# A fused mLSTM cell and feed-forward kernel: another order for the first chunk, the first weight quarter converted in halves, and 60 spare products

## The chip, the cores and the metric

The kernel runs on one core of one Trainium2 chip. A core has TensorE (PE: matrix products, with its weight loads shown as PEld), VectorE (DVE), ScalarE (ACT), GpSimd (POOL) and SyncE (SP), which here does nothing but issue DMAs. The metric is the device time of one execution in microseconds (us). Before the change the median of three runs is 491.05 us (490.83 to 491.35).

## The reference

Two layers follow each other. The first is an mLSTM cell: 4 batches, 8 heads, 768 time steps, head dimension 40. The second is a feed-forward block on its output, 3072 rows of 320 values.

```python
for t in range(S):
    m_new = max(f[t] + m, i[t])
    f_stab = exp(f[t] + m - m_new); i_stab = exp(i[t] - m_new); m = m_new
    C = f_stab * C + i_stab * outer(v[t], k[t])
    n = f_stab * n + i_stab * k[t]
    h = C @ q[t]
    y[t] = sigmoid(o[t]) * h / max(abs(n . q[t]), 1)
...
x = y.transpose(0, 2, 1, 3).reshape(B * S, H * D)
h = x @ w_in
out = max(0.01 * h, h) @ w_out
```

`w_in` is 320 x 2048 and `w_out` 2048 x 320. In this kernel both arrive as 64-bit floating point numbers and are converted on the chip.

## The kernel before

The 768 time steps are cut into six chunks of 128 (called c or g, 0 to 5); a step s is one batch of one chunk, s = 4c + b. Inside a chunk the cell is done with products: scores of k and q, a mask of decay factors from the gates, values, and the state that goes on to the next chunk. Each chunk's output (four steps of 128 rows) is one group for the feed-forward block. While group g goes through the feed-forward block, the cell of chunk g + 1 is worked in between its units.

Chunk 0 has nothing to be hidden behind. Its order is written out by hand in the string `ORDER` (lines 1102 to 1119), which `first_chunk` (line 1121) reads item by item. Inside `tc.manual_schedule` (line 1152) each of PE, DVE, ACT and POOL executes its instructions in the order in which the program issues them, and SP's queue has the program's order too. The items, with the batch as their first number:

- `ld`: load k, q, v (SP, line 368). `lo`: load the output gate (line 397). `lw n`: load piece n of the weights (line 230 for `w_in`, line 235 for `w_out`).
- `g`, `ge`, `ug`: the gates' scans on DVE (lines 293 to 313), their exponentials on ACT (319 to 325), their transposition on PE into the bank `tg` (342, 347), copied by DVE (352, 354).
- `ab n`: spread the gate sums over the partitions, two batches at once (PE, 461); `abw`: add the causal mask (DVE, 471); `exp`: eight exponentials of 128 x 128 (ACT, 488).
- `tr b i`, `tc b i`: transpose k (i = 0) or q (i = 1) on PE (578), copy the result on ACT (584). `sc`: scores (PE, 593); `scm`: multiply them into the mask (DVE, 600).
- `vu`: v times gate (POOL, 498); `st`: the state's products (PE, 608); `stc`: its copy (DVE, 616).
- `val`: values, eight products of 41 columns into the bank `pa` (PE, 673); `den`: denominators (DVE, 665 to 667); `o`: tanh of the output gate (ACT, 524); `gate`: gate times values (DVE, 685); `gp`: scaling by the denominators (POOL, 702).
- `x`: transpose the result (PE, 876, 877); `xc`: copy it to `xT` in four pieces (ACT, 889, 890).
- `nw n`: one further step of converting weight piece n. `narrow_weights` (line 248) is a generator: its first step is an absolute value on ACT (260), and six steps on DVE follow (262, 264, 266, 271, 275, 277).
- `ff n`: a unit of the feed-forward block (products at line 907, leaky relu on ACT at 915).
- `warm n`: n products of the identity with itself into one bank, whose result nobody reads (336).
- `fd s`: load of a step of chunk 1 (`load` and `spread`, lines 370, 377, 440); `ll s i`: a late part of it (411); `ps`, `tiles`: memsets on POOL.

PE writes into eight PSUM banks: four with the tag "mm" (pool `psf`: `warm`, `ab`, `ph`, `po`) and four with the tag "c" (pool `psc`: `tkq`, `sc`, `dC`, `pa`, `tg`, `xt` and the cell's). A bank is given out in turn, and its first writer waits for the last reader of the use before.

`w_in` is kept as four quarters (n = 0 to 3), each 128 partitions x 1280 and each loaded by ten DMAs; quarter n serves the feed-forward's pairs of row blocks j = 2n and 2n + 1, of which the even one uses the first and the odd one the second 128 columns of each of the five slots of 256. `w_out` is kept as eight pieces (n = 4 to 11) of 128 x 640. Quarters 0 and 1 lie, before their conversion, in parts of `acts` not yet in use, quarters 2 and 3 in `raw_t`.

Behind `first_chunk` stands a loop over the feed-forward units of group 0 (lines 1153 to 1200). For unit i it first takes `PASSES[i]` steps of weight conversion (pieces 2 to 11), asks for further pieces of `w_out` by `fetch`, issues the unit, and then as many units of chunk 1's cell as `place` says: the m-th of them goes behind unit `place[m]`. The units of the cell are, for each batch, `u_parts` (lines 634 to 661: scores and the state of the chunk's halves, `sd`) and `u_plain` (706 to 730: the values, bank `hN` at line 713), then the gates of chunk 2 between them, and last `u_x1` for the four batches. After this loop groups 1 to 5 follow, from line 1276 on.

In group 0 the feed-forward units before are fourteen half units of 256 columns (two batches) behind the two of the first chunk, then sixteen parts of the second product (`part`, line 938: four products of 320 columns), 30 in all.

Of the kernel before, what the change touches and what calls it, by code (L numbers as in the profile page):

```python
# [22 lines left out]
def kernel(  # L23
# [27 lines left out]
    B, H, S, D = q.shape  # L51
    P = 128
# [15 lines left out]
    NF = FF // P  # L68
    GT = B * P
    KF = Dm // P  # L70
    KR = Dm - KF * P
    KC = Dm // DP
# [4 lines left out]
    gp = ctx.enter_context(tc.tile_pool(name="gates", bufs=1))  # L77
# [96 lines left out]
    def f_of(r, j):  # L174
        n, e = divmod(j, 2)
        return 4 * n + 2 * r + e
# [8 lines left out]
    raws = {}  # L185
# [51 lines left out]
    def halves(n, size):  # L237

        flat = late_t[:].rearrange("p n t -> p (n t)")
        if n < QN:  # L240
            at = flat[:, n % 2 * (WC // 2) :]
        elif n % 2 == 0:
            at = xb[:].rearrange("p n d -> p (n d)")
        else:
            at = flat[:, 2 * H * SL :]
        return at[:, : size // 2].bitcast(BF16)

    def narrow_weights(n):

        if not wide:
            return
        raw, dst = raws.pop(n)
        words = raw.bitcast(U32).rearrange("p (c two) -> p c two", two=2)
        lo, hi = words[:, :, 0], words[:, :, 1]
        tops = raw.bitcast(BF16).rearrange("p (c four) -> p c four", four=4)[:, :, 3]
        top = halves(n, dst.shape[1])
        t = top.bitcast(U16)
        nc.scalar.activation(top, tops, AF.Abs)  # L260
        yield
        nc.vector.tensor_scalar(top, top, scalar1=2.0**-15, scalar2=130560.0, op0=ALU.max, op1=ALU.min)
        yield
        nc.vector.tensor_scalar(t, t, scalar1=0x07F0, scalar2=3, op0=ALU.bitwise_and, op1=ALU.logical_shift_left)
        yield
        nc.vector.scalar_tensor_tensor(  # L266
            t, in0=tops.bitcast(U16), scalar=0xC000, in1=t, op0=ALU.bitwise_and, op1=ALU.bitwise_or,
        )
        yield
        d = dst.bitcast(U32)  # L270
        nc.vector.tensor_scalar(
            d, hi, scalar1=0x000FFFFF, scalar2=0x00100000, op0=ALU.bitwise_and, op1=ALU.bitwise_or,
        )
        yield
        nc.vector.scalar_tensor_tensor(dst, in0=lo, scalar=2.0**-32, in1=d, op0=ALU.mult, op1=ALU.add)  # L275
        yield
        nc.vector.scalar_tensor_tensor(dst, in0=dst, scalar=2.0**-20, in1=top, op0=ALU.mult, op1=ALU.mult)
# [78 lines left out]
    st = {}  # L356
# [540 lines left out]
    def by_slot(t, dt=F32):  # L897
        return t[:].bitcast(dt).rearrange("p b (k t) -> p k b t", t=P)

    def ff_units(g):  # L900
        xT = by_slot(st["xT", g])

        def rows(j, ph, cols, slots):
            bs = slice(cols.start // P, cols.stop // P)
            for slot in slots:
                for r in range(2):
                    nc.tensor.matmul(  # L907
                        ph[r][:, cols], lhsT=w_row(r, slot, j), rhs=xT[DP * r : DP * (r + 1), slot, bs, :],
                        start=(slot == 0), stop=(slot == KC - 1),
                    )  # L910

        def relu(j, ph, cols):
            for r in range(2):
                f = f_of(r, j)
                nc.scalar.activation(acts[:, f, cols], ph[r][:, cols], AF.Prelu, alpha=0.01)  # L915

        def pair(j):
            ph = []

            def first():  # L920
                ph.extend(psf.tile([P, GT], F32, name=f"ph{r}", tag="mm") for r in range(2))
                rows(j, ph, slice(0, GT), range(3))

            def second():
                rows(j, ph, slice(0, GT), range(3, KC))
                relu(j, ph, slice(0, GT))

            return [first, second]

        def half(j, h):  # L930
            ph = [psf.tile([P, GT], F32, name=f"ph{r}", tag="mm") for r in range(2)]
            cols = slice(h * GT // 2, (h + 1) * GT // 2)
            rows(j, ph, cols, range(KC))
            relu(j, ph, cols)

        po = {}

        def part(n, m):
            if m == 0:
                po[n] = psf.tile([P, Dm], F32, name="po", tag="mm")  # L940
            for f in range(m * NF // 4, (m + 1) * NF // 4):
                nc.tensor.matmul(  # L942
                    po[n][:], lhsT=acts[:, f, ts(n, P)], rhs=w_out[:, f, :], start=(f == 0), stop=(f == NF - 1),
                )
            if m == 3:
                if n < 2:
                    y = wk.tile([P, Dm], F32, name="y")[:]
                else:
                    y = wk.tile([P, H, D1], F32, name="hn")[:].rearrange("p h d -> p (h d)")[:, :Dm]
                nc.scalar.copy(y, po[n][:])  # L950
                nc.sync.dma_start(out[n * S + g * P : n * S + (g + 1) * P, :], y)

        if g == 0:

            ins = [(j, h) for j0 in range(0, NF // 2, 2) for h in range(2) for j in (j0, j0 + 1)]
            return [lambda j=j, h=h: half(j, h) for j, h in ins] + [
                lambda n=n, m=m: part(n, m) for m in range(4) for n in range(B)
            ]
        firsts = [u for j in range(NF // 2) for u in pair(j)]
        for n in range(2):  # L960
            firsts[KH + 2 * n] = lambda n=n, u=firsts[KH + 2 * n]: (u(), mix_early(n))
        return firsts, fast_units(g)
# [137 lines left out]
            nc.tensor.matmul(st["warm"][:], lhsT=ident[:], rhs=ident[:], start=True, stop=True)  # L1100

    ORDER = """
ld 0; warm 12; ld 1; ld 2; lo 0; lo 1; lo 2; lw 0
g 0; ld 3; lw 1; lw 2; lo 3; ge 0; ug 0; tr 0 0
tr 0 1; vu 1; vu 0; tc 0 0; ab 0; abw 0; tr 1 0; tc 0 1
exp 0; sc 0; abw 1; tr 1 1; tc 1 1; st 0; tc 1 0; exp 1
st 1; scm 0; stc 1; stc 0; ab 2; tiles; g 1; abw 3
sc 1; scm 1; ge 1; abw 2; val 0; tr 2 0; tr 2 1; val 1
o 1; den 0; tc 2 1; gate 1; ps 1; tc 2 0; o 0; exp 2
gate 0; gp 0; ug 1; sc 2; scm 2; x 0; tr 3 0; nw 0  # L1110
nw 0; vu 2; den 1; gp 1; nw 0; nw 0; nw 0; exp 3
tr 3 1; tc 3 0; ps 0; st 2; tc 3 1; xc 0; val 2; vu 3
sc 3; stc 2; nw 0; o 2; nw 0; nw 1; scm 3; den 2
x 1; xc 1; gate 2; st 3; o 3; gp 2; nw 1; nw 1
stc 3; nw 1; ff 0; val 3; den 3; x 2; gate 3; fd 4
nw 1; ps 3; xc 2; ff 1; gp 3; x 3; nw 1; ll 4 1
xc 3; ps 2; ll 4 2; fd 5; ll 5 1; lw 3; lw 4; lw 5
lw 6; fd 6; fd 7; ll 5 2; nw 1
"""

    def first_chunk():

        ffs, narrow = [], {}

        def ff(n):
            if not ffs:
                ffs.extend(ff_units(0))
            ffs[n]()

        def step(n):  # L1130
            if n not in narrow:
                narrow[n] = narrow_weights(n)
            next(narrow[n], None)
# [15 lines left out]
        return ffs  # L1149

    E = mybir.EngineType
    with tc.manual_schedule(engines={E.PE, E.DVE, E.Activation, E.Pool}):
        ffs = first_chunk()[2:]
        fetch = {6: (3, 4), 17: (7,), 10: (5, 6)}
        PASSES = (3, 2, 1, 0, 3, 5, 3, 1, 0, 1, 4, 2, 3, 4, 1, 2, 8, 4, 5, 4, 5, 4, 0, 7, 3, 5, 5, 1, 2, 8)
        place = (1, 4, 7, 9, 11, 15, 15, 18, 23, 25, 27, 27, 28)
        late = {}
        now = (None for n in range(2, QN + NF // 2) for _ in narrow_weights(n))

# [170 lines left out]
```

## Time and profile before

| | |
|---|---|
| median of three runs | 491.05 us (490.83 to 491.35) |
| the profiled execution: time | 491.28 us |
| its span, first to last instruction | 489.4 us |
| mean granted clock of PE | 0.982 |
| first chunk ends on PE (last transpose of x) | 47.1 us |
| first product of group 1 | 135.24 us |

The page gives each engine's busy time as a share of the span, then the span in 40 equal slices of 12.2 us: a digit is the busy share of a slice in tenths, and in the row PEclk the granted clock of PE. Views of the trace are named in words: the table by stretch gives busy time, number of records, clock and DMA of each engine between two times; the waits say what an engine's idle time ended with; the chain follows the work that ended last back from its end; the timeline lists groups of an engine's instructions with their start and length in us, and in brackets the idle time before them and what ended it. A product of 32-bit numbers shows as two records on PE.

### The profile page before, as it was taken

The page shows a single profiled execution, that of the slowest core. Times are in us where ns is not written, and L with a number is a line of the kernel's source. Part 1 is how long each engine was busy: PE and PEld are TensorE (multiplying, and loading weights), DVE is VectorE, ACT ScalarE, POOL GpSimd, SP SyncE. Part 2 cuts the span into 40 slices and gives each one's busy share as a digit, 9 for nine tenths or more (in the row PEclk, how much of TensorE's full clock was granted, in tenths as well). Part 3 has the DMA queues.
Part 4 walks back from the last instruction along what each step waited for, and adds up shares of the span by engine and source line. Part 5 has one row for each costly group of instructions (what it writes and reads, how often), then busy time and mean ns, then how long its engine had stood idle before and what let it go on. Part 6 is the DMA issues. An engine that isn't in the chain of part 4 may idle for free.

```text
span 489.4 us, 12856 instructions
## 1 busy us (share of the span) xinstructions
PE 476.1 (97%) x5137; PEld 377.9 (77%) x5137; DVE 365.9 (75%) x595; ACT 197.4 (40%) x510; POOL 160.3 (33%) x207
## 2 busy tenths in 40 slices
PE   7969998999999999999999999999999999999997
PEld 6857887777745479975559995557998889988997
DVE  5796999799924999777898777679899968335611
ACT  4674885453642240324342141425024752156310
POOL 4234454070600725817280563644220002100020
PEclk9867999999999999999999999999999999999999
DMA  7777686898623566668787877755151030100001
GB/s 136 177 191 146 161 226 134 216 229 177 143 97 90 133 158 176 162 152 202 152 197 160 189 181 177 184 144 153 44 229 42 1 107 1 42 15 0 1 1 54
DMA packets 142699, 63.41 MB, mean 130 GB/s; under 512 B 110832, under 2 KB 130864, under 8 KB 142640
## 3 DMA queue, kind: packets, MB, share of 16 engines
q1 hardware_dynamic: 142256, 62.47, 52.7%
q8 instruction: 40, 0.66, 0.6%
q14 instruction: 19, 0.16, 0.1%
q10 hardware_dynamic: 384, 0.13, 0.1%
HBM read 51.68 MB, written 8.27 MB: 122 GB/s over the span
## 4 chain that ended last, share of the span: by engine, by line
PE 82%; SPq 8%; DVE 5%; issue 2%; DMA 2%; ACT 1%; ACTq 0%; DVEq 0%
PE po L983 32%; PE ph L907 24%; PE ph L833 8%; PE po L942 6%; PE pe L833 4%; PE pT L743 3%; PE sd L650 3%; SPq L230 3%; SPq L368 2%; SPq L377 1%; PE sd L655 1%; DVE w_in L275 1%; PE hN L713 1%; DMA raw<-in_moe_w_in_dram 1%; DVE late L266 1%
## 5 line engine op out<-in xcount | busy, mean ns | idle before, releaser
L907 PE MATMUL ph<-xT,w_in 64*128 64x512 f32 (+1 forms) x800 | 146.3, 516 | 0.2 <-ACT xT L889 0.2
L907 PEld LDWEIGHTS ph<-xT,w_in 64*128 64x128 f32 x800 | 77.8, 190 | 57.4 <-issue 50.8
L983 PE MATMUL po<-w_out,acts 128*128 128x160 f32 x640 | 91.0, 301 | 0.0
L983 PEld LDWEIGHTS po<-w_out,acts 128*128 128x128 f32 x640 | 87.5, 190 | 3.4 <-ACT w L488 1.5
L915 ACT ACTIVATE acts<-ph 128x512 f32<-128x512 f32 (+1 forms) x80 | 36.8, 508 | 83.6 <-PE ph L907 83.5
L488 ACT ACTIVATE w<-w,gT 128x64 f32<-128x64 f32 (+1 forms) x192 | 52.0, 349 | 29.0 <-POOL w L480 28.0
L628 POOL TENSOR_TENSOR S<-S,f 40x336 f32<-40x336 f32 x36 | 32.5, 902 | 93.3 <-PE pT L743 49.5
L983 PE MATMUL po<-raw,acts 128*128 128x160 f32 x320 | 45.1, 299 | 0.0
L983 PEld LDWEIGHTS po<-raw,acts 128*128 128x128 f32 x320 | 44.0, 190 | 0.0
L660 DVE TENSOR_TENSOR qn<-w,sd 64x512 f32<-64x512 f32 x40 | 27.4, 684 | 21.0 <-PE sd L655 14.0
L1016 POOL TENSOR_TENSOR y<-y,raw 128x160 f32<-128x160 f32 x10 | 5.5, 555 | 112.3 <-ACT y L1015 112.3
L942 PE MATMUL po<-w_out,acts 128*128 128x320 f32 x128 | 36.0, 436 | 0.0
L855 DVE SCALAR_TENSOR_TENSOR acts<-ph,acts 128x512 f32<-128x512 f32 x32 | 20.6, 684 | 20.7 <-ACT acts L853 20.7
L541 DVE TENSOR_TENSOR qn<-kqT,late 64x512 f32<-64x512 f32 x32 | 33.1, 1033 | 1.0
L480 POOL TENSOR_TENSOR w<-w,i 128x512 f32<-128x512 f32 x20 | 31.8, 1591 | 2.7 <-ACT acts L915 1.9
L942 PEld LDWEIGHTS po<-w_out,acts 128*128 128x128 f32 x128 | 23.8, 190 | 9.5 <-issue 0.3
L757 POOL TENSOR_TENSOR xb<-xb,den 128x320 f32<-128x320 f32 x16 | 11.6, 727 | 48.7 <-DVE xb L754 48.7
L853 ACT ACTIVATE acts<-pe 128x512 f32<-128x512 f32 x32 | 17.4, 594 | 19.2 <-PE pe L833 19.0
L761 DVE STREAM_TRANSPOSE x<-xb 128x512 f32<-128x512 f32 x16 | 17.8, 1114 | 7.7 <-POOL xb L757 7.7
L859 ACT ACTIVATE acts<-acts 128x512 f32<-128x512 f32 x32 | 19.7, 633 | 8.0 <-DVE acts L855 8.0
L983 PE MATMUL po<-raw 128*128 128x160 f32 x160 | 22.7, 300 | 0.0
L650 PEld LDWEIGHTS sd<-kqT 40*64 40x64 f32 x640 | 19.7, 135 | 3.7 <-issue 3.0
(166 smaller groups left out, 773.2 us busy)
## 6 DMA issues: line engine op xcount, KB each, us to landing
w<-a_dr SPq DMA_DIRECT2D x40, 128.0 KB, 3.7
rb<-in_k_dram SPq DMA_DIRECT2D x64, 80.0 KB, 3.1
rb<-in_q_dram SPq DMA_DIRECT2D x64, 80.0 KB, 2.7
rb<-in_o_gate_dram SPq DMA_DIRECT2D x64, 80.0 KB, 2.6
xT<-x_dr SPq DMA_DIRECT2D x32, 160.0 KB, 3.2
late<-a_dr SPq DMA_DIRECT2D x32, 128.0 KB, 3.4
x_dr<-x SPq DMA_DIRECT2D x16, 256.0 KB, 3.4
kn<-in_k_dram SPq DMA_DIRECT2D x24, 160.0 KB, 3.7
```

Source lines behind the costliest of these rows:

```text
L480: nc.gpsimd.tensor_tensor(w, w, cm2.unsqueeze(1).to_broadcast([P, H, SL]), op=ALU.add)
L488: yield nc.scalar.activation(w[:, h, :], w[:, h, :], AF.Exp, bias=gT[c][:, 0, bh : bh + 1], scale=1.0)
L541: nc.vector.tensor_tensor(mixed(s)[rows, 1 - r], d["kqT"][rows, 1].rearrange("p (h t) -> p h t", t=SL), d["ea"][rows], op=ALU.mult,)
L628: nc.gpsimd.tensor_tensor(new, old, g, op=ALU.mult)
L650: nc.tensor.matmul(bank[1 - u][toks, h, :], lhsT=kqT[rows, 0, ts(h, SL)], rhs=kqT[rows, 1, ts(h, SL)], start=True, stop=True,)
L660: nc.vector.tensor_tensor(mixed(s)[toks, u], w[toks], bank[1 - u][toks], op=ALU.mult)
L833: nc.tensor.matmul(ph[r][:], lhsT=parts["w", key][n][part, at : at + P], rhs=xs[key][part, slot, :], start=start and slot == 0, stop=stop ...
L855: nc.vector.scalar_tensor_tensor(fs[r], in0=ph[r][:], scalar=1.0 + EPS, in1=fs[r], op0=ALU.mult, op1=ALU.add,)
L907: nc.tensor.matmul(ph[r][:, cols], lhsT=w_row(r, slot, j), rhs=xT[DP * r : DP * (r + 1), slot, bs, :], start=(slot == 0), stop=(slot == KC ...
L915: nc.scalar.activation(acts[:, f, cols], ph[r][:, cols], AF.Prelu, alpha=0.01)
L942: nc.tensor.matmul(po[n][:], lhsT=acts[:, f, ts(n, P)], rhs=w_out[:, f, :], start=(f == 0), stop=(f == NF - 1),)
L983: nc.tensor.matmul(bank[:], lhsT=left[:, f, :], rhs=right[:, f, :], start=f == 0, stop=f == KH - 1)
```

## The change

The order of the first chunk is written anew, in four respects.

- Loads. The first quarter of `w_in` (`lw 0`) stands behind the loads of steps 0 and 1 and their output gates; before it stood behind those of steps 0 to 2. Loads of steps 2 and 3 follow it. The other three quarters are asked for later or earlier among the loads of chunk 1: quarter 1 ahead of `fd 4`, quarter 2 behind it, quarter 3 ahead of `fd 5`; before quarters 1 and 2 stood ahead of `fd 4` and quarter 3 behind `fd 5`.
- Conversion. `narrow_weights` takes a second argument e. With it, it converts the 128 columns of each slot that the even (e = 0) or odd (e = 1) block uses, 640 of 1280 columns. Quarter 0 is converted so, in two series of seven steps; quarter 1 as a whole, as before.
- Spare products. 60 in 23 groups, 13 of them ahead of the first gate transposition and 47 behind it; before there were 12 in one group.
- Feed-forward. `half(j, h)` becomes `some(j, b0, b1)` with any range of batches. In the first chunk stand, as before, j = 0 and j = 1 over the batches 0 and 1. Behind it follow j = 0 and 1 over the batches 2 and 3, and then j = 2 to 7 over all four batches, each as a `pair` of two units (three slots, then two slots and the relu) with 512 columns; then the sixteen parts. Again 30 units. In group 0 there are 100 products at line 907 instead of 160, over as many columns in all.

`PASSES`, `place` and `fetch` have new numbers to go with these units.

```diff
-    def narrow_weights(n):
+    def narrow_weights(n, e=None):
...
-        raw, dst = raws.pop(n)
+        raw, dst = raws[n]
...
         top = halves(n, dst.shape[1])
+        if e is not None:
+            lo, hi, tops, top, dst = (
+                a.rearrange("p (k e t) -> p e k t", k=KC, t=P)[:, e] for a in (lo, hi, tops, top, dst)
+            )
...
-        def half(j, h):
+        def some(j, b0, b1):
+
             ph = [psf.tile([P, GT], F32, name=f"ph{r}", tag="mm") for r in range(2)]
-            cols = slice(h * GT // 2, (h + 1) * GT // 2)
+            cols = slice(b0 * P, b1 * P)
             rows(j, ph, cols, range(KC))
             relu(j, ph, cols)
...
-            ins = [(j, h) for j0 in range(0, NF // 2, 2) for h in range(2) for j in (j0, j0 + 1)]
-            return [lambda j=j, h=h: half(j, h) for j, h in ins] + [
-                lambda n=n, m=m: part(n, m) for m in range(4) for n in range(B)
-            ]
+            ins = [lambda j=j: some(j, 2, B) for j in range(2)] + [u for j in range(2, NF // 2) for u in pair(j)]
+            return some, ins + [lambda n=n, m=m: part(n, m) for m in range(4) for n in range(B)]
...
     ORDER = """
-ld 0; warm 12; ld 1; ld 2; lo 0; lo 1; lo 2; lw 0
-g 0; ld 3; lw 1; lw 2; lo 3; ge 0; ug 0; tr 0 0
-tr 0 1; vu 1; vu 0; tc 0 0; ab 0; abw 0; tr 1 0; tc 0 1
-exp 0; sc 0; abw 1; tr 1 1; tc 1 1; st 0; tc 1 0; exp 1
-st 1; scm 0; stc 1; stc 0; ab 2; tiles; g 1; abw 3
-sc 1; scm 1; ge 1; abw 2; val 0; tr 2 0; tr 2 1; val 1
-o 1; den 0; tc 2 1; gate 1; ps 1; tc 2 0; o 0; exp 2
-gate 0; gp 0; ug 1; sc 2; scm 2; x 0; tr 3 0; nw 0
-nw 0; vu 2; den 1; gp 1; nw 0; nw 0; nw 0; exp 3
-tr 3 1; tc 3 0; ps 0; st 2; tc 3 1; xc 0; val 2; vu 3
-sc 3; stc 2; nw 0; o 2; nw 0; nw 1; scm 3; den 2
-x 1; xc 1; gate 2; st 3; o 3; gp 2; nw 1; nw 1
-stc 3; nw 1; ff 0; val 3; den 3; x 2; gate 3; fd 4
-nw 1; ps 3; xc 2; ff 1; gp 3; x 3; nw 1; ll 4 1
-xc 3; ps 2; ll 4 2; fd 5; ll 5 1; lw 3; lw 4; lw 5
-lw 6; fd 6; fd 7; ll 5 2; nw 1
+warm 3; warm 4; g 0; ld 0; ld 1; ge 0; lo 0; lo 1
+lw 0; ld 2; warm 3; warm 1; warm 2; ug 0; warm 4; lo 2
+ab 0; tr 1 0; tr 0 0; tc 1 0; tc 0 0; ld 3; tr 0 1; abw 0
+abw 1; warm 1; tc 0 1; tr 1 1; warm 4; vu 0; sc 0; warm 1
+lo 3; warm 1; st 0; vu 1; tc 1 1; exp 0; scm 0; o 0
+exp 1; stc 0; st 1; stc 1; warm 4; warm 1; sc 1; warm 7
+ab 2; scm 1; val 0; abw 3; g 1; tr 2 0; tc 2 0; ge 1
+o 1; val 1; tr 2 1; den 0; gate 0; tc 2 1; abw 2; tr 3 0
+vu 2; tiles; ps 1; gate 1; exp 2; warm 5; sc 2; vu 3
+gp 0; scm 2; nw 0 0; den 1; nw 0 0; warm 3; warm 2; nw 0 1
+nw 0 0; nw 0 1; ug 1; tr 3 1; tc 3 0; o 2; x 0; warm 1
+warm 3; val 2; xc 0; nw 0 1; tc 3 1; exp 3; nw 0 0; warm 4
+nw 0 0; st 2; sc 3; den 2; nw 0 1; stc 2; gate 2; st 3
+gp 1; nw 0 0; scm 3; nw 0 0; x 1; warm 2; gp 2; ps 0
+lw 1; fd 4; ll 4 1; lw 2; warm 2; warm 1; val 3; stc 3
+nw 0 1; xc 1; o 3; den 3; nw 1; gate 3; nw 0 1; nw 0 1
+nw 1; ps 2; ps 3; x 2; gp 3; nw 1; ff 0 0 2; ll 4 2
+lw 3; fd 5; lw 4; ll 5 1; nw 1; x 3; warm 1; xc 3
+xc 2; lw 5; fd 6; nw 1; nw 1; nw 1; fd 7; ll 5 2
+ff 1 0 2; lw 6
 """
...
-        fetch = {6: (3, 4), 17: (7,), 10: (5, 6)}
-        PASSES = (3, 2, 1, 0, 3, 5, 3, 1, 0, 1, 4, 2, 3, 4, 1, 2, 8, 4, 5, 4, 5, 4, 0, 7, 3, 5, 5, 1, 2, 8)
-        place = (1, 4, 7, 9, 11, 15, 15, 18, 23, 25, 27, 27, 28)
+        fetch = {10: (5, 6), 19: (7,), 8: (3, 4)}
+        PASSES = (6, 2, 3, 1, 0, 2, 3, 1, 5, 1, 0, 2, 3, 1, 10, 1, 1, 2, 1, 3, 2, 9, 2, 4, 4, 1, 7, 2, 0, 17)
+        place = (1, 6, 11, 13, 16, 18, 19, 20, 23, 24, 24, 25, 27)
```

More of the change, by code (lines that the diff above doesn't have):

```diff
@@ L1123, in first_chunk, with ff, step @@
         ffs, narrow = [], {}
-        def ff(n):
+        def ff(j, b0, b1):
             if not ffs:
                 ffs.extend(ff_units(0))
[L1128 to L1133, printed above, removed]
+            ffs[0](j, b0, b1)
+        def step(n, e=None):
+            if (n, e) not in narrow:
+                narrow[n, e] = narrow_weights(n, e)
+            next(narrow[n, e], None)
         acts_of = {
@@ L1148, in first_chunk @@
                     acts_of[name](*map(int, args))
-        return ffs
+        return ffs[1]
     E = mybir.EngineType
     with tc.manual_schedule(engines={E.PE, E.DVE, E.Activation, E.Pool}):
-        ffs = first_chunk()[2:]
-        fetch = {6: (3, 4), 17: (7,), 10: (5, 6)}
-        PASSES = (3, 2, 1, 0, 3, 5, 3, 1, 0, 1, 4, 2, 3, 4, 1, 2, 8, 4, 5, 4, 5, 4, 0, 7, 3, 5, 5, 1, 2, 8)
-        place = (1, 4, 7, 9, 11, 15, 15, 18, 23, 25, 27, 27, 28)
+        ffs = first_chunk()
+        fetch = {10: (5, 6), 19: (7,), 8: (3, 4)}
+        PASSES = (6, 2, 3, 1, 0, 2, 3, 1, 5, 1, 0, 2, 3, 1, 10, 1, 1, 2, 1, 3, 2, 9, 2, 4, 4, 1, 7, 2, 0, 17)
+        place = (1, 6, 11, 13, 16, 18, 19, 20, 23, 24, 24, 25, 27)
         late = {}
```

## The prediction

> **What bounds the kernel now.** I read the page's engine shares first, then the slices, the busy time by stretch, the chain of waits, and last the timelines of the first chunk, engine by engine.
>
> ```profile
> PE 476.1 (97%) x5137; PEld 377.9 (77%) x5137; DVE 365.9 (75%) x595; ACT 197.4 (40%) x510; POOL 160.3 (33%) x207
> ...
> PEclk9867999999999999999999999999999999999999
> ```
>
> TensorE (PE) is busy for 97% of the 489.4 us, so a gain can only come from its few idle or slowed places. The clock row says where it is slowed: slices 2 to 4, the first chunk. The table by stretch (the stretch and its length, busy time of PE, PEld, DVE, ACT and POOL, then clock, DMA share, GB/s) is cut where the granted clock changes.
>
> ```profile
> 1.46:4.36 2.90, 2.90 (x13) 2.90 (x14) 1.09 (x6) 0.00 (x0) 2.55 (x8) 1.00 0.30 68
> 4.36:5.77 1.41, 1.41 (x13) 1.22 (x11) 0.94 (x3) 1.02 (x1) 0.69 (x2) 1.00 1.17 222
> 5.77:18.01 12.24, 10.26 (x167) 8.79 (x166) 8.83 (x29) 8.92 (x27) 2.81 (x9) 1.00 0.94 175
> 18.01:21.42 3.41, 2.63 (x22) 2.40 (x23) 3.09 (x10) 1.88 (x5) 0.00 (x0) 1.00 0.70 200
> 21.42:28.25 6.83, 6.83 (x50) 5.99 (x50) 4.66 (x12) 5.38 (x16) 3.38 (x7) 0.50 0.77 161
> 28.25:31.66 3.41, 2.88 (x35) 2.71 (x33) 3.33 (x5) 3.21 (x8) 2.37 (x5) 1.00 0.75 210
> 31.66:41.90 10.24, 6.98 (x49) 5.03 (x45) 8.48 (x13) 3.50 (x6) 1.31 (x2) 0.50 0.74 185
> 47.09:135.24 88.15, 86.06 (x1196) 68.64 (x1195) 81.67 (x115) 53.21 (x139) 38.85 (x36) 1.00 0.80 184
> 135.24:486.20 350.96, 350.96 (x3570) 276.04 (x3570) 249.94 (x398) 117.52 (x306) 105.14 (x128) 1.00 0.44 112
> ```
>
> Three stages are seen. From 135.24 (first product of group 1) PE never idles: nothing here is changed, and whatever comes earlier shifts the end one for one. From 47.09 (end of the first chunk) to 135.24 PE misses 88.15 - 86.06 = 2.1 us, while VectorE (DVE) is busy 93%. Before 47.09 lies what the change reorders: clock at half for 6.83 and for 10.24 us, and PE idle for 1.98 + 0.78 + 0.53 + 3.26 = 6.55 us.
>
> The waits of PE in the second stage (total, times, longest) name its holes:
>
> ```profile
> PE hN L713 <- DVE S L632: 1.0, 1, 1.0
> PE tg L342 <- DVE hn L724: 0.4, 1, 0.4
> PE hN L713 <- DVE qn L660: 0.3, 1, 0.3
> ```
>
> PE waits there for DVE, which still converts weights beside the cell of chunk 1. The chain says through what:
>
> ```profile
> 12.97 1.06 SPq L230
> ...
> 24.55 2.51 DMA acts<-in_moe_w_in_dram
> ...
> 58.60 2.85 DMA raw<-in_moe_w_in_dram
> 61.70 1.40 ACT late L260
> ```
>
> The w_in quarters, asked for one instruction after another on SP's queue, are on the chain at their asking and at their landing.
>
> **The change part by part.** The timelines (start, length) from which the replay below is made; PE's first:
>
> ```profile
> 7.74 1.17 PE L461 MATMUL ab<-a,ident 32*128 32x128 f32 x32
> ...
> 17.34 0.63 PE L578 MATMUL tkq<-ident,kn 128*128 128x128 f32 x4
> ...
> 19.39 1.98 PE L673 MATMUL pa<-S,w 128*128 128x41 f32 x16
> ...
> 36.74 0.79 PE L608 MATMUL dC<-vu,kn 128*40 128x42 f32 x16 [3.26 <-ACT xT L890]
> 37.45 4.61 PE L907 MATMUL ph<-xT,w_in 64*128 64x256 f32 x20
> ...
> 44.26 2.43 PE L907 MATMUL ph<-xT,w_in 64*128 64x256 f32 x20
> ...
> 46.89 0.27 PE L877 MATMUL xt<-ident,x 128*64 128x128 f32 x1
> ```
>
> *Spare products.* 24 records of 12 products are in the first two stretches: 13 records in 2.90 us are 0.22 a record at the slow start, and at full clock 11 more take 1.41 us, 0.13 a record, so 0.25 us a product (two records). Thirteen now stand before the gate transposes instead of twelve: the added 0.25 us fits the 0.34 us between 5.77 and the first gate transpose at 6.11, so 0. The other 47 cost 47 x 0.25 = 11.75 us of PE. What can pay for it: PE's 6.55 us of idle time, and the slow stretches, whose 6.83 + 6.98 = 13.81 us of busy time would take half at full clock, a gain of 6.9. Together 13.45 - 11.75 = 1.7: if the clock never falls and PE never waits, the first chunk ends at 45.4, 1.7 earlier. That is one bound. The other is that they stand in front of useful work.
>
> *The replay* of the new order with the durations of before, engine by engine. DVE and ACT give these:
>
> ```profile
> 9.00 2.74 DVE L471 TENSOR_TENSOR w<-ab,cmask 128x256 f32<-128x256 f32 x8 [1.95 <-PE ab L461]
> ...
> 16.73 1.42 DVE L471 TENSOR_TENSOR w<-ab,cmask 128x256 f32<-128x256 f32 x4
> ...
> 33.00 1.49 DVE L277 SCALAR_TENSOR_TENSOR w_in<-w_in,late 128x1280 f32<-128x1280 f32 x1
> ...
> 47.91 2.44 DVE L277 SCALAR_TENSOR_TENSOR w_in<-w_in,late 128x1280 f32<-128x1280 f32 x1
> ```
>
> ```profile
> 7.41 1.07 ACT L584 COPY kqT<-tkq 128x512 f32<-128x512 f32 x2 [0.92 <-PE tkq L578]
> ...
> 9.46 2.56 ACT L488 ACTIVATE w<-w,gT 128x128 f32<-128x128 f32 x8 [0.97 <-DVE w L471]
> ...
> 24.75 1.37 ACT L260 ACTIVATE late<-acts 128x1280 bf16<-128x1280 bf16 x1 [1.45 <-issue]
> ```
>
> The four spares ahead of ab 0 take the place of the two transpose groups that stood there (same 1.0 us), so the mask adds keep 9.00 to 11.75. One later spare takes the first ab bank and waits for five of those eight adds (9.0 + 5 x 0.34 = 10.7); behind it is the last transpose of batch 1, and ACT's copy of that is ahead of exp 0, which so starts at 12.2 instead of 9.46. Twelve spares and ab 2 follow scores 1: ab 2 ends at 20.2, so the second pair of mask adds starts there and not at 16.73, with DVE idle for 1.5 us. From 20.2 to 25.4 PE has values 0, values 1 and three transpose groups, and no spare. Then five spares and scores 2 (to 27.9), the gate transposes at 29.9, x 0 at 30.9, values 2 until 33.75, x 1 at 37.05 (its bank is values 2's, free when gate 2 has read it), values 3 at 40.3, x 2 at 40.75. Quarter 0 converts in halves on DVE meanwhile: even half ready at 39.5, odd half at 43.55. So ff 0 runs from 40.75 (before: from 37.45, at half clock for 4.61 us), x 3 to 43.5, ff 1 from 43.75 to 46.05. PE ends the chunk at 46.0 against 47.09: **-1.1**. The 0.6 us beside the bound of 45.4 are waits for DVE.
>
> *Halves.* Six more DVE instructions and one more ACT. Two halves have as many elements as the whole; L277 on 1280 elements takes 1.49, and a 128 x 128 exponential of exp 0 takes 0.32, so a further instruction has a floor well below that. I take 0.1 each, 0.6 on DVE, inside the replay; between 0 and 6 x 0.3 = 1.8.
>
> *The loads.* SP's rows, then a k load's usual time to landing:
>
> ```profile
> 12.97 7.66 SPq L230 DMA_DIRECT2D acts<-in_moe_w_in_dram  x10
> 20.68 0.59 SPq L368 DMA_DIRECT2D kn<-in_k_dram  x1
> ...
> 51.34 7.86 SPq L230 DMA_DIRECT2D raw<-in_moe_w_in_dram  x10
> ```
>
> ```profile
> kn<-in_k_dram SPq DMA_DIRECT2D x24, 160.0 KB, 3.7
> ```
>
> The first quarter's ten DMAs move past load 2 and o 2 and start near 9.3, not 12.97. Nothing comes of the 3.7 us: on ACT its first step still stands behind exp 2 (27.85 in the replay, against 24.75). Load 2 pays: kn asked at 17.5 to 18.0 lands near 21.6, and transposes 2 need it at 22.0; load 3 lands and is needed near 25. Slack about 0.5 and 0, so 0 taken, +1 as the other end. Quarter 1 lands near 34, needed near 39. Quarter 2 now goes behind chunk 1's first feed: asked from 37.2, landed 46.3, wanted by ACT at 47.8. Quarter 3 goes ahead of the second feed: asked from 44.2 instead of 51.34, landed near 53 instead of 61.45. The chain's steps at 58.60 and 61.70 go; next late is DVE alone.
>
> *Behind the first chunk.* DVE ends quarter 1 at 51.0 in the replay, against 47.91 + 2.44 = 50.35. That is 0.65 later, with PE 1.1 earlier. But the first units are ordered otherwise: the second batch's hN stands behind two units of 256 columns and twelve of 512 (2 x 2.26 + 6 x 4.5 = 31.5 us of feed-forward) where before there were ten of 256 (22.6); the price of 4.5 is that of a pair in the chain:
>
> ```profile
> 81.27 4.52 PE ph L907 x40
> ```
>
> So DVE has 9 us more before the 1.0 us hole's place: in the replay it gets there at 82 to 85, PE at 85, and the hole becomes 0 to 0.5. Later the fourth round of w_out products needs quarter 11 of the weights (DVE 121 to 124.5) when PE arrives at 123 to 124: up to 0.8 of a new hole. I take 1.2 us of holes for 2.1: **-0.9**, between -1.8 (0.3 left) and 0.
>
> Sum: -1.1 - 0.9 = -2.0. The profiled run took 491.28 (1.9 over its span, 0.23 over the median), so 489.3; span 487.4.
>
> **The clock: row and rule.** In the rows the clock fell at 21.42 after a stretch in which PE was busy for 2.63 of 3.41 us, most of it values (1.98) and thin transposes, and rose at 28.25. The Trainium skill, "TensorE: Matmul & The Clock Gate", Part 4 (PE-mode transpose), says that transposes don't count as busy for the clock. By it the stretch from 20.2 to 25.4, more than half transposes, would be idle and the clock would halve: the second rival's 492.7. The trace speaks against the rule: in the stretch below, eight records of transposes took 1.91 us, those of x 0 stood beside them, and the clock rose at its end.
>
> ```profile
> 24.84:28.25 3.41, 1.91 (x8) 1.70 (x8) 0.00 (x0) 0.50 0.77 175
> ```
>
> **The rivals.**
> 1. *DVE sets the end, PE's gain turns into waits.* For it: DVE's 81.67 of 88.15 us; it ends quarter 1 no earlier (51.0 for 50.35), with the same work behind. Against: the holes before were only 2.1 us, and the longest had DVE work that the new order gives 9 us to. If all that DVE loses shows and no hole closes: 491.28 + 0.65 = 491.9, and 491.0 where a hole closes: no change.
> 2. *The clock still falls, in the stretch without spares.* From 20.2 to 25.4 PE has only values, whose 41 columns are thin, and transposes, much like 17.34 to 21.37 before (two transpose groups and one values), after which it fell. Against: there 0.78 us were idle, here none, by the replay. If it falls at about 24.8 it stays for 6.83 or 10.24 us, and half of that is lost: +3.4 to +5.1 on 489.3, so 492.7 to 494.4: slower. It decides as soon as the row for 24.8 to 31.7 shows 0.50. Of its chance, 0.05 is for the rule of transposes.
> 3. *Spares in front of useful work.* If each bank wait and drain makes a spare cost 0.31 for 0.25, 47 of them add 2.8; or load 2 and 3 land a microsecond late behind the quarter. Either makes the first chunk end at 48 to 49 on both engines: 492.1 to 493.
>
> **How the numbers follow.** A measurement of this kernel tells 0.2%, about 1 us: faster is below 490.07, slower above 492.03. Forecast 0.48, at 489.3, its own range 487.8 (first chunk at 45.4 and 0.3 of holes) to 490.0 (a hole back). Rival 1 0.20, rival 2 0.20, rival 3 0.12. So faster 0.48, same 0.20, slower 0.32. The range runs from 487.2, where the halves cost nothing too, to 492.8, which leaves out the upper half of rivals 2 and 3.
>
> **What would show it.** Clock: no 5 to 8 in the PEclk row after slice 1. Spares: 0.25 each, exp 0 at 12.2, the second mask pair at 20.2. ff 0 starts near 40.8 and ff 1 ends near 46. Quarter 1 is done near 51; quarter 3 has landed by 53 and no L260 waits for it. The hN hole on S is under 0.6; group 1 starts near 133.3. Wrong if the clock row shows a half after 21, if PE ends the chunk after 47.1, or if holes from there to group 1 are above 2.1 us.

## The result, and the profile after

The changed kernel takes 487.06 us (median of four runs, 486.61 to 487.46), the kernel before beside it 490.94 (489.29 to 491.35): ratio 0.9925, 95% interval 0.9908 to 0.9942. That is 3.9 us or 0.75% faster, 0.14 us below the low end of the range and about twice the gain that was forecast. Faster was the forecast and faster it is; where the time came from is only half of what the prediction said. The profiled execution has a span of 484.5 us against 489.4. On the page of the changed kernel, the engines' shares and the rows of PE and its clock in the 40 slices:

```profile
PE 478.6 (99%) x5113; PEld 371.8 (77%) x5113; DVE 364.6 (75%) x601; ACT 196.1 (40%) x499; POOL 159.4 (33%) x207
...
PE   8999999999999999999999999999999999999997
...
PEclk9999999999999999999999999999999999999999
```

PE is busy for 99% and its clock does not fall any more. The table by stretch of the changed kernel (stretch and length, busy time of PE, PEld, DVE, ACT, POOL, then clock, DMA share, GB/s):

```profile
19.27:25.43 6.16, 6.16 (x78) 5.91 (x77) 4.83 (x17) 2.27 (x7) 2.87 (x9) 1.00 0.99 164
25.43:45.96 20.53, 20.33 (x209) 18.20 (x208) 18.25 (x40) 16.00 (x40) 10.97 (x19) 1.00 0.80 181
45.96:130.77 84.81, 84.81 (x1076) 56.28 (x1075) 79.63 (x116) 53.53 (x130) 34.24 (x33) 1.00 0.78 180
130.77:480.88 350.11, 350.11 (x3571) 275.75 (x3570) 251.65 (x399) 115.48 (x301) 105.34 (x129) 1.00 0.47 115
```

Three sums can be made against the kernel before. PE ends the first chunk at 45.96 instead of 47.09: -1.13. From there to group 1 it takes 84.81 us instead of 88.15: -3.34, with no idle time left in it. And group 1 itself is shorter, which nobody had on the list: in the timeline of PE, first of the kernel before and then of the changed one, the first products of group 1 and of group 2 are

```profile
135.24 1.12 PE L907 MATMUL ph<-xT,w_in 64*128 64x512 f32 x2 [0.22 <-ACT xT L889]
...
215.22 0.70 PE L907 MATMUL ph<-xT,w_in 64*128 64x512 f32 x2
```

```profile
130.77 0.70 PE L909 MATMUL ph<-xT,w_in 64*128 64x512 f32 x2
...
209.89 0.70 PE L909 MATMUL ph<-xT,w_in 64*128 64x512 f32 x2
```

215.22 - 135.24 = 79.98 before, 209.89 - 130.77 = 79.12 after: -0.86. Before, the first two records took 1.12 us instead of 0.70: PE waited there for ACT's copies to `xT`, as `x_late` below shows. The first 60 records took 14.01 us before and take 13.15 now, so the first pair has half of the 0.86, and the other half is lost by the end of these 60. Of the 5.33 us, 0.4 come back behind the last product (from PE's end to the end of the span 3.2 us before, 3.6 after). The profiled execution before was one of its slower ones (491.28), hence 4.9 us in the spans and 3.9 in the medians.

### The profile page after: what moved, and what is told of

The parts are those of the page before. It is cut to its first block, busy times and chain, and to the rows that moved or that the text cites. A ratio compares the mean times of both kernels' runs of the same rounds, so it can differ in the third digit from the quotient of the medians.

```text
span 484.5 us, 12804 instructions
## 1 busy us (share of the span) xinstructions
PE 478.6 (99%) x5113; PEld 371.8 (77%) x5113; DVE 364.6 (75%) x601; ACT 196.1 (40%) x499; POOL 159.4 (33%) x207
## 4 chain that ended last, share of the span: by engine, by line
PE 95%; DVE 1%; issue 0%; POOL 0%; POOLq 0%; DVEq 0%
PE po L984 32%; PE ph L909 29%; PE ph L835 8%; PE po L945 7%; PE pe L835 4%; PE pT L745 3%; PE sd L652 3%; PE warm L338 2%; PE pa L675 1%; PE sd L657 1%; PE hN L715 1%; PE tk L566 1%; PE tq L552 1%; PE sc L595 1%; PE tkq L580 0%; PE tg L349 0%
## 5 line engine op out<-in xcount | busy, mean ns | idle before, releaser
L909 PE MATMUL ph<-xT,w_in 64*128 64x512 f32 (+1 forms) x680 | 142.3, 569 | 0.0
L909 PEld LDWEIGHTS ph<-xT,w_in 64*128 64x128 f32 x680 | 64.5, 187 | 66.1 <-issue 63.7
L917 ACT ACTIVATE acts<-ph 128x512 f32<-128x512 f32 (+1 forms) x68 | 35.1, 567 | 80.3 <-PE ph L909 80.1
L630 POOL TENSOR_TENSOR S<-S,f 40x336 f32<-40x336 f32 x36 | 33.9, 941 | 81.2 <-PE pT L745 47.3
```

Of the source, the lines that this page charges most:

```text
L630: nc.gpsimd.tensor_tensor(new, old, g, op=ALU.mult)
L909: nc.tensor.matmul(ph[r][:, cols], lhsT=w_row(r, slot, j), rhs=xT[DP * r : DP * (r + 1), slot, bs, :], start=(slot == 0), stop=(slot == KC ...
```

## The experiments

The numbers to compare with are 487.06 and, timed again below, 487.26 for the changed kernel; the kernel before had medians of 489.85 to 490.26 beside the experiments.

**Which half brings it.** The new first chunk with the old units behind it, and the reverse.

```diff
 # new_first_old_rest: in the changed kernel
-            ins = [lambda j=j: some(j, 2, B) for j in range(2)] + [u for j in range(2, NF // 2) for u in pair(j)]
+            ins = [... some(j, 2 * h, 2 * h + 2) for j0 in range(0, NF // 2, 2) for h in range(2) for j in (j0, j0 + 1)][2:]
-        fetch, PASSES, place of the changed kernel
+        fetch, PASSES, place of the kernel before
 # old_first_new_rest: in the changed kernel
-    ORDER = (the new one)
+    ORDER = (the old one, ff 0 and ff 1 written as ff 0 0 2 and ff 1 0 2)
```

> The new first chunk, with the units, conversion steps, fetches and places of before behind it. Theory (the 3.3 us that the stage behind the first chunk lost come from the units' order and width, not from the first chunk): the first chunk ends on PE at 46.0 as in the changed kernel, the stage from there to group 1 takes 87.5 to 89 us with 1.5 to 3 us of waits for DVE, and the time is 490 to 491.5. Rival (the earlier landing of quarter 3, which the new order of loads brings, closed the holes): the stage takes 86 us or less, waits under 0.5 us, time 488 to 488.7.

> The first chunk's order of before (12 spare products, loads and whole quarters as before), with the new units, conversion steps, fetches and places behind it. Theory (units): PE ends the first chunk at 47.1, the stage behind it takes 84.9 to 85.5 us, time 488.0 to 488.8. Rival (loads): quarter 3 lands at 61 again, PE waits over 1 us for DVE in the stage, which takes 86.5 us or more, time 489.5 or more.

Neither half gains anything alone. The first takes 492.07 us (ratio to before 1.0031, interval 1.0013 to 1.0049), the second 492.36 (1.0040, 1.0014 to 1.0066). In the first, PE ends the first chunk at 45.8 and the stage behind it takes 88.75 us; the waits of PE in it:

```profile
PE hN L715 <- DVE S L634: 1.0, 1, 1.0
PE tk L566 <- DMA rb<-in_q_dram: 0.9, 1, 0.9
PE tg L344 <- DVE hn L726: 0.4, 1, 0.4
PE hN L715 <- DVE qn L662: 0.3, 1, 0.3
PE ph L909 <- ACT xT L891: 0.2, 1, 0.2
```

These are the holes of the kernel before, with 0.9 us for a load (`tk`) where it had 0.2, and this although quarter 3 lands early: with the old units the first chunk's gain turns into waits. The theory held, its time was exceeded by 0.6. The profile can't show all of that: it is of an execution that took 490.80 us, the least of the ten, with a mean granted clock of 1.000, while the nine others had 0.996 to 0.999. A mean of 0.997 over 490 us is some 3 us at half clock, which costs 1.5 us (an estimate); where the clock fell, no trace shows. In the second kernel the rival came true, with ACT where it had named DVE. Its timelines of ACT and SP:

```profile
60.54 1.33 ACT L262 ACTIVATE late<-raw 128x1280 bf16<-128x1280 bf16 x1 [8.43 <-DMA raw<-in_moe_w_in_dram]
```

```profile
50.07 8.15 SPq L230 DMA_DIRECT2D raw<-in_moe_w_in_dram  x10
```

Quarter 3 is asked for at 50.07 as before, but the new list of conversion steps wants it early. ACT stands in front of its first step for 8.43 us with the relus behind it. PE waits 4.4 us for them, up to 62.91, the clock is at 0.50 from 61.51 to 68.33, and the stage takes 93.6 us.

**The one load.** In the changed kernel, only quarter 3 goes back behind the feed of step 5; then, in the old first chunk, only that quarter goes ahead of it.

```diff
 # lw3_late
-lw 3; fd 5; lw 4; ll 5 1; nw 1; x 3; warm 1; xc 3
+fd 5; lw 3; lw 4; ll 5 1; nw 1; x 3; warm 1; xc 3
 # old_first_lw3_early: in old_first_new_rest
-xc 3; ps 2; ll 4 2; fd 5; ll 5 1; lw 3; lw 4; lw 5
+xc 3; ps 2; ll 4 2; lw 3; fd 5; ll 5 1; lw 4; lw 5
```

> The changed kernel with one item moved: quarter 3 of w_in is asked for behind the feed of step 5, as before, not ahead of it. Theory (the new order of the units rests on that quarter landing early): it lands near 59 to 61, its first step on ACT, wanted at 53.7, waits for it for 4 us or more with the relus behind it, PE waits 2 to 4.5 us for ACT, time 489.5 to 491.5. Rival (the order and width of the units alone closed the holes): no wait of PE over 0.5 us, time 487.0 to 487.8.

> The first chunk's order of before with one item moved, quarter 3 of w_in asked for ahead of the feed of step 5, and the new units, conversion steps, fetches and places behind it. Theory (the new units need nothing of the new first chunk but that quarter early; spare products bring only a steadier clock): no wait of PE over 0.5 us behind the first chunk, that stage takes 84.8 to 85.5 us, PE ends the first chunk between 44.5 and 47.5 by how often the clock falls, time 486.5 to 489. Rival (the new first chunk's order or spares are needed too): a wait over 1 us stays in the stage, or the first chunk ends after 48, time 489.5 or more.

Both mechanisms came as the theories had them, but the time with the quarter late is 1.5 us over its range: 492.97 us (ratio 1.0066, 1.0041 to 1.0090). PE's wait behind the first chunk, ACT's wait in front of it, and the stretch behind PE's wait in the table by stretch:

```profile
PE ph L909 <- ACT acts L917: 3.1, 1, 3.1
```

```profile
58.58 1.35 ACT L262 ACTIVATE late<-raw 128x1280 bf16<-128x1280 bf16 x1 [6.10 <-DMA raw<-in_moe_w_in_dram]
```

```profile
62.34:65.76 3.42, 3.42 (x11) 2.62 (x9) 2.70 (x5) 3.02 (x10) 0.00 (x0) 0.50 0.75 119
```

So the wait of 3.1 us is not the whole cost: the 3.42 us at half clock behind it cost half of their length, 1.7, more. This profile is of the execution with the least time of six, 491.44 us at a mean clock of 0.996; the other five had 0.992 to 0.997.

With the old first chunk and the quarter early: 487.97 us (0.9945, 0.9923 to 0.9967), no wait of PE in the stage, which takes 85.24 us. So some 2.3 us of the gain come from what is new behind the first chunk (units, conversion steps, fetches and places together) with one load moved. The rest of the new first chunk, spare products, halves and all, is worth 0.7 us on top (487.97 against 487.26), and as the two intervals overlap, this is not clear of the noise. Its clock, though, still falls in the first chunk:

```profile
PEclk9858999999999999999999999999999999999999
```

**The spare products.** All 47 behind the first gate transposition are taken out.

```diff
 # no_spares: in ORDER, each "warm n" behind "ug 0" is gone, for example
-exp 1; stc 0; st 1; stc 1; warm 4; warm 1; sc 1; warm 7
+exp 1; stc 0; st 1; stc 1; sc 1
```

> The changed kernel without its 47 spare products behind the first gate transposition. Theory (they hold the clock, and this is worth more than they cost): the granted clock falls to 0.50 for at least 6.8 us between 18 and 45 us, PE ends the first chunk at 47 to 49, time 488 to 490.5. Rival (they only fill time that PE has, or stand in the way): PE ends the first chunk at 45.0 to 45.9 and the time is 486 to 487.

The time is 492.18 us (ratio to before 1.0037, 1.0014 to 1.0060), above the theory's range, as is the end of the first chunk below. In its table by stretch and its waits of PE in the first chunk:

```profile
17.37:28.80 11.43, 11.43 (x64) 10.92 (x60) 6.02 (x20) 4.51 (x15) 4.33 (x12) 0.50 0.90 186
28.80:49.86 21.06, 20.23 (x125) 17.19 (x123) 16.77 (x36) 10.96 (x26) 9.31 (x15) 0.51 0.71 177
```

```profile
PE sc L595 <- DVE w L602: 1.3, 1, 1.3
PE tg L344 <- DVE w L602: 0.8, 1, 0.8
PE tkq L580 <- DMA kn<-in_k_dram: 0.4, 1, 0.4
PE sc L595 <- ACT kqT L586: 0.3, 1, 0.3
```

The clock stays at half for more than 30 us, although PE counts as busy all through the first of these stretches, and PE ends the first chunk at 52.2. The spares' 11.75 us buy 6.3 there, by the two profiles, and about 5 in the medians. In this order of work they are needed; the old order, with twelve, had 17 us at half clock in the profile of before.

**The width of the units.** Pairs of 512 columns become two units of 256 at the same places.

```diff
 # narrow_units
-[u for j in range(2, NF // 2) for u in pair(j)]
+[lambda j=j, b=b: some(j, b, b + 2) for j in range(2, NF // 2) for b in (0, 2)]
```

> The changed kernel, but each pair of units of 512 columns for j = 2 to 7 is two units of 256 columns (batches 0 and 1, then 2 and 3) at the same two places. Theory (a part of the stage's gain is the width): the stage takes 85.7 to 86.2 us instead of 84.8, without waits for DVE, time 487.8 to 488.4. Rival (the width costs nothing, all of the gain is from waits): the stage takes 84.8 to 85.1, time 486.8 to 487.4.

487.77 us (0.9947, 0.9929 to 0.9965), 0.03 under the theory's range. The stage's row, 0.05 under it:

```profile
46.68:132.33 85.65, 85.51 (x1197) 68.88 (x1195) 79.45 (x116) 54.39 (x142) 33.64 (x33) 1.00 0.75 177
```

85.65 against 84.81, without a wait for DVE: the width is worth 0.84 us, with 121 fewer PE records over the same columns.

**The copies for group 1.**

```diff
 # x_late
-        place = (1, 6, 11, 13, 16, 18, 19, 20, 23, 24, 24, 25, 27)
+        place = (1, 6, 11, 13, 16, 18, 19, 20, 23, 25, 27, 27, 28)
```

> The changed kernel with the last four cell units (transposes and copies of chunk 1's result) behind the units 25, 27, 27, 28 as before, not 24, 24, 25, 27. Theory (0.9 us of the gain is that ACT's copies to xT are done when group 1 starts): the first products of group 1 wait again for the last copies, the distance from the first product of group 1 to the first of group 2 is 79.6 to 80.0 us instead of 79.1 and the product itself starts 0.2 to 0.4 late, time 487.6 to 488.4. Rival: the copies are hidden anyway, time 486.8 to 487.4.

487.69 us (0.9952, 0.9934 to 0.9970). The first products of groups 1 and 2 in its timeline of PE:

```profile
131.75 1.12 PE L909 MATMUL ph<-xT,w_in 64*128 64x512 f32 x2 [0.22 <-ACT xT L891]
...
211.73 0.70 PE L909 MATMUL ph<-xT,w_in 64*128 64x512 f32 x2
```

The distance is 79.98 us again, the first two records take 1.12 and the first 60 take 14.01, each to the hundredth as in the kernel before: the theory held.

**The halves.**

```diff
 # whole_q0: in ORDER, "nw 0 0" becomes "nw 0" and each "nw 0 1" is gone
-gp 0; scm 2; nw 0 0; den 1; nw 0 0; warm 3; warm 2; nw 0 1
+gp 0; scm 2; nw 0; den 1; nw 0; warm 3; warm 2
```

> The changed kernel with quarter 0 converted as a whole, its seven steps where the even half's stood, none for the odd half. Theory (the halves let the first feed-forward unit start before the odd half is done): scores 3 and values 3 come about 1.1 us later on DVE and PE, ff 0 starts at 41.3 to 41.8 instead of 40.3, PE ends the first chunk at 46.5 to 47.1, time 487.5 to 488.3. Rival (the halves only add seven instructions): PE ends the first chunk at 45.9 or before, quarter 1 is done before 51.5, time 486.4 to 487.2.

487.14 us (0.9950, 0.9928 to 0.9971), the time of the changed kernel. The first unit did start late, at 41.25 instead of 40.31, though 0.4 of this is a later start (the first spreading at 8.19 for 7.76); PE ended the chunk at 46.67, or some 46.2 without that, and quarter 1 was done at 51.4, as the rival had it. The chunk's end as measured is the theory's, the time the rival's: the halves bring the first unit forward by half a microsecond, quarter 1 is done 0.75 us later with them (52.15), and no difference in time is left.

**Moving and dropping spares.** In the changed kernel DVE waits 1.5 us in front of the second pair of mask adds:

```profile
20.46 1.42 DVE L473 TENSOR_TENSOR w<-ab,cmask 128x256 f32<-128x256 f32 x4 [1.50 <-PE ab L463]
```

Seven spares stand in front of the products it waits for. They were moved, together with a single spare further ahead, and then dropped.

```diff
 # spares_moved
-abw 1; warm 1; tc 0 1; tr 1 1; warm 4;
+abw 1; tc 0 1; tr 1 1; warm 1; warm 4;
-sc 1; warm 7
-ab 2; scm 1; val 0;
+sc 1
+ab 2; scm 1; val 0; warm 7;
 # no_warm7
-sc 1; warm 7
+sc 1
```

> The changed kernel with two groups of spare products moved, none left out: the one ahead of the second transpose of batch 1, which waits 0.4 us for a bank, goes behind it; the seven ahead of the second spreading of the gate sums go behind values 0. Theory (those stand in front of work that DVE waits for 1.5 us): the second pair of mask adds starts 1.3 to 1.8 us earlier, near 18.8, PE ends the first chunk at 44.5 to 45.4, time 485.5 to 486.6. Rival 1 (the load of step 2 or the exponentials of batch 2 take the wait's place): PE ends the first chunk at 45.7 to 46.2, time within 0.4 of the changed kernel. Rival 2 (the clock falls in the stretch from 17.5): 489 or more.

> The changed kernel without the seven spare products ahead of the second spreading of the gate sums; the other 53 stay, in their places. Theory (these seven are in front of work that DVE waits for 1.5 us): the second pair of mask adds starts 1.4 to 1.8 us earlier, PE ends the first chunk 0.7 to 1.5 us earlier against its first gate transposition, time 485.6 to 486.6. Rival 1 (loads of steps 2 and 3, or the exponentials of batch 2, set the end): 0 to 0.4 us earlier. Rival 2 (they hold the clock): the granted clock falls between 18 and 28, time 488 or more.

Moved, they cost 4.9 us: 491.99 us (1.0054, 1.0027 to 1.0082). The mask adds do start earlier, as the theory had it: at 19.53, against 21.40 in the profile of `changed_again`, whose first gate transposition is as late. But there is a wait that neither the theory nor a rival of this run had. The timeline of PE, and a row of its table by stretch:

```profile
24.42 3.10 PE L338 MATMUL warm<-ident 128*128 128x128 f32 x14 [3.17 <-DVE w L473]
```

```profile
24.67:28.08 3.41, 3.41 (x18) 3.41 (x18) 0.59 (x2) 0.00 (x0) 0.00 (x0) 0.50 0.82 190
```

`ab` takes all four "mm" banks, so a spare behind it gets a bank that DVE empties only with the mask add of the second batch, and everything on PE stands behind that. The wait is 3.17 us, and the half clock behind it, which the second rival had without the wait, costs another 1.7. The prediction's replay has a wait of this kind behind the first `ab`, where it measured 0.41 us. A product that computes nothing still needs a bank.

Dropped, they bring about 1.0 us: 486.23 us (0.9908, 0.9887 to 0.9929) beside 487.26 for the changed kernel in the same comparison; the two intervals overlap, so this is not clear of the noise. The clock holds. PE ends the first chunk at 45.79, 0.94 earlier than the changed kernel beside it, of which 0.21 is an earlier first gate transposition. Its profile shows what comes late next, in the timelines of PE and ACT:

```profile
24.91 0.63 PE L580 MATMUL tkq<-ident,kn 128*128 128x128 f32 x4 [1.00 <-DMA kn<-in_k_dram]
```

```profile
56.32 1.40 ACT L262 ACTIVATE late<-raw 128x1280 bf16<-128x1280 bf16 x1 [3.07 <-DMA S<-in_v_dram]
```

The load of step 3 is late by 1.0 us, and again quarter 3: the row names the DMA that came last by the profile, but what the step reads is quarter 3, whose tenth DMA landed at 56.06 (53.49 in the changed kernel). That DMA took 3.9 us from asking to landing, against 2.8 in the changed kernel, so a part of the wait is this execution's own. PE lost 0.9 us by it. This profiled execution took 488.04 us, the three others 485.85 to 486.53.

**The changed kernel again**, as it is, beside the two kernels `no_warm7` and `old_first_lw3_early`.

> The changed kernel itself once more, timed beside the two that follow. Theory (its clock never falls, so that only the moment at which the clock first rises differs from run to run): all times between 486.5 and 488, spread under 1.5 us, the kernel before beside it over 2.5 us. Rival (the spread is the chip's, not the kernel's): both spreads are alike.

486.70 to 487.42 over four runs, a spread of 0.7 us; before beside it 489.26 to 491.31, 2.1 us, less than expected, but in the other comparisons it had 3.3 to 4.1 over 11 to 31 runs. Three profiles have the first chunk in its order of before. Its own, with half clock for 17 us, ends it at 47.09, `old_first_lw3_early`, with 20 us, at 46.57, and `old_first_new_rest`, with 10 us, at 45.05. The changed kernel ends it at 45.96 in the profile after and at 46.73 here. What moves in it is the start: its 26 records of spare products ahead of the gate transposition took 4.66 us in the profile after and 5.92 here. The trace's record of the clock begins, at full clock, at 4.63 us there and at 7.50 here; the views count what is ahead of that as 1.00.

```profile
1.47 5.92 PE L338 MATMUL warm<-ident 128*128 128x128 f32 x26 [1.47 <-POOL ident masks.py:199]
```

**One load earlier as well.** The seven spares dropped, and quarter 3 asked for one DMA sooner.

```diff
 # no_warm7_lw3: in no_warm7
-nw 1; ps 2; ps 3; x 2; gp 3; nw 1; ff 0 0 2; ll 4 2
-lw 3; fd 5; lw 4; ll 5 1; nw 1; x 3; warm 1; xc 3
+nw 1; ps 2; ps 3; x 2; gp 3; nw 1; ff 0 0 2; lw 3
+ll 4 2; fd 5; lw 4; ll 5 1; nw 1; x 3; warm 1; xc 3
```

> As the kernel without the seven spare products, and quarter 3 of w_in is asked for ahead of the late load of step 4 (its output gate), not behind it. Theory (with the first chunk earlier, that quarter's landing is what comes late next, and ACT waited for it with the relus behind it): ACT's wait in front of quarter 3's first step is under 2.4 us instead of 3.1, PE's wait behind it under 0.4 us instead of 0.9, time 485.7 to 486.3, the lowest of all. Rival (one DMA less ahead of ten is within the scatter of their issue): wait and time as without it, 486.0 to 486.8.

485.50 us (six runs, 485.06 to 486.35; ratio to before 0.9904, 0.9874 to 0.9934): every run is below every run of the changed kernel, and the median is a little below the theory's range. Against `no_warm7` the intervals overlap. ACT's wait is half of the one shown there, which was of the execution at 488.04, and PE's behind it is gone, so what the moved load adds by itself is not clear of the noise:

```profile
53.90 1.42 ACT L262 ACTIVATE late<-raw 128x1280 bf16<-128x1280 bf16 x1 [1.45 <-DMA raw<-in_moe_w_in_dram]
```

## Why the prediction was right, and where it was not

*The first chunk* (forecast -1.1, ending at 46.0; measured -1.13, 45.96). The replay held step by step. PE's and ACT's timelines of the changed kernel:

```profile
19.27 1.28 PE L463 MATMUL ab<-a,ident 32*128 32x128 f32 x32
20.48 1.98 PE L675 MATMUL pa<-S,w 128*128 128x41 f32 x16
22.29 0.64 PE L580 MATMUL tkq<-ident,kn 128*128 128x128 f32 x4
22.76 1.88 PE L675 MATMUL pa<-S,w 128*128 128x41 f32 x16
24.47 0.63 PE L580 MATMUL tkq<-ident,qn 128*128 128x128 f32 x4
24.94 0.60 PE L580 MATMUL tkq<-ident,kn 128*128 128x128 f32 x4
...
40.31 2.43 PE L909 MATMUL ph<-xT,w_in 64*128 64x256 f32 x20
...
43.60 2.43 PE L909 MATMUL ph<-xT,w_in 64*128 64x256 f32 x20
```

```profile
12.33 2.44 ACT L490 ACTIVATE w<-w,gT 128x128 f32<-128x128 f32 x8
```

Exponentials 0 at 12.33 (12.2 forecast), the spreading done at 20.5 (20.2), ff 0 at 40.31 (40.75), ff 1's end at 46.0 (46.05). Quarter 1 was done at 52.15, 1.1 later than the replay's 51.0, and it did not matter. That the end came out at -1.13 is partly luck, though: it is one profiled execution against one. The three profiles of the old order end between 45.05 and 47.09, and against the lowest nothing is won. How much the new first chunk gains by itself is not shown; `old_first_lw3_early` leaves it 0.7 us, within the noise.

*The halves* at 0.6 us of DVE, inside the replay: no difference in time either way, as `whole_q0` shows.

*The loads*: quarter 0's early landing bought nothing, as forecast. That quarter 3 must land early was in the sum as a wait that goes ("next late is DVE alone"); this step failed by size. `lw3_late` shows that it carries the whole gain and more: 5.7 to 5.9 us are lost without it, in its profile 3.1 as a wait of PE and 1.7 as half clock. The quarter landed at 53.49, near the 53 of the forecast, but against the sign given ACT did wait for it, 1.11 us up to 53.75, without a wait of PE. It, not DVE, is next late, as `no_warm7` shows.

*Behind the first chunk* (forecast -0.9; measured -3.34 and, inside group 1, another -0.86). Two steps failed. First, the width was put at nothing: a pair of 512 columns was priced at 4.5, which is two halves at 2.26, and the run with narrow units measures 0.84 us for it. The rest of the 3.34 is, by subtraction, 2.5 us of waits: all of the 2.1 that the kernel before had by the difference of length and busy time, and 0.4 that this difference did not show. The 1.2 us that were left in the forecast did not come. Both of the replay's candidates came out on their good side: DVE's state sum ends at 83.02 when PE arrives at 83.87, and piece 11 of the weights is done at 121.56 when the fourth round starts at 121.9. The new units need quarter 3 early for this (`lw3_late`), and with the old units the waits stay although it is early (`new_first_old_rest`); which of units, conversion steps, fetches and places closes them was not tested apart. Second, the sentence that from 135.24 PE never idles was read off a busy time that contains waiting products; the copies for group 1, which the new `place` does sooner, were worth 0.86 us, and `x_late` brings them back exactly.

*The rivals.* DVE as the bound: not here, as PE waits nowhere; but with the old units behind the new first chunk this is what happens. Spares in front of work: true for seven of them (some 1.0 us, within the noise), not for their sum. The clock: it held through the stretch without spares, 19.27 to 25.43 above, at 1.00, which decides against that rival. The prediction called this stretch more than half transposes; by the starts of the rows above, the three groups of transposes fill 1.4 of its 6.16 us and the values, whose products are thin, 3.5. So the stretch does not test the rule of the Trainium skill, "TensorE: Matmul & The Clock Gate", Part 4 (PE-mode transpose), that transposes do not count as busy for the clock. Against that rule there is only the rise at 28.25 in the kernel before, which the prediction shows.

## What to carry to other kernels

A stage in which PE is nearly always busy can still hide microseconds: compare the length of like products at the start of a stage with the same ones later, since a wait inside a pair counts as busy. When an order, a list of conversion steps and a load's place are changed together, test each alone; here each half made the kernel slower by itself, and one load moved past another made the difference. A wait of about 3 us can cost more than its length, as the half clock behind it shows in three profiles here. Filler work is costed in what it holds up (a bank, the engine's queue), not only in its own time.

## What the runs showed of the hardware

The clock does not follow PE's busy time alone. In the kernel without spares it stayed at 0.50 through 11.43 us in which PE was busy throughout, with products of 41 columns, transposes and scores, and idle for at most 1.33 us at a stretch behind its first products. The Trainium skill, "TensorE: Matmul & The Clock Gate", section "Why this matters for your kernels", asks for no idle gaps over about 3 us; that was kept here and was not enough, so the measurement decides. What the 47 products of 128 x 128 change there is how full the array is. That it is the fill that counts, and how much of it is needed, is argued from these rows and was not measured by itself.

A wait counts too. Behind 3.09 us without a product in `lw3_late` the clock was at half for 3.42 us, behind 3.17 us in `spares_moved` for 3.41, and around the end of 4.43 us in `old_first_new_rest` for 6.82. Between the first and the last product, the stretches at half clock in the profiles of this case last 3.41, 6.83, 10.24, 17.07 or 34.13 us, whole multiples of the first.
